# Whole-slot weight conversion on VectorE and attention in 64-token halves, in a gated linear attention and two MoE layers

## The chip, the cores and the metric

The kernel runs on one core of one Trainium2 chip. The metric is the device time of one execution in microseconds (us), as the median of several runs. Times of single instructions come from one profiled execution.

## What is computed

A gated linear attention over 4 batches, 8 heads, 768 tokens and a head size of 48 gives 3072 tokens of 384 values; then come two feed-forward layers with 1536 hidden values each. Cut to what matters:

```python
f = 1.0 / (1.0 + np.exp(-f_logit))
for t in range(S):
    state = f[:, :, t, :, None] * state + np.einsum('bhd,bhe->bhde', k[:, :, t], v[:, :, t])
    y[:, :, t] = np.einsum('bhd,bhde->bhe', q[:, :, t], state)
x = y.transpose(0, 2, 1, 3).reshape(B * S, H * D)
a = x @ w_a;  b = x @ w_b;  x1 = a * b @ w_out
g = x1 @ w_gate;  val = x1 @ w_val
out = g * (1.0 / (1.0 + np.exp(-g))) * val @ w_out2
```

The weights reach the kernel as float64 bit patterns in int64.

## The kernel before, in words

**Two phases of six blocks.** A block is 512 tokens. Phase 1 (`ph` 0) runs the first MoE layer on blocks 0 to 5, phase 2 (`ph` 1) the second. A block runs over 12 slices `j` of 128 hidden values. For a slice TensorE (PE) does three groups of 9 matmuls of 512 columns: `g_in(j, a)`, `g_in(j, b)` and, one slice late, `g_out(j-1)`. Nine, because each operand is held as a rounded part `hi` and a remainder `lo`, and hi·hi, hi·lo and lo·hi are taken for three pieces of 128 rows. `g_in(j, a)` ends with a copy to `a_sb` on ScalarE (ACT), a Silu in phase 2 (L535). `g_in(j, b)` ends with the product on VectorE (DVE, L539). Then ACT rounds the product to `h_hi` (L511) and DVE takes the remainder `h_lo` (L513). `g_out` reads both; its second matmul is the first that reads `h_lo` (L557, L558, L559 are its three lines). After slice 11 the three accumulators are copied out and stored (L568), to `x1d` in phase 1, to `out` in phase 2. Phase 2 loads `x1d` back and splits it (`x1_split`, L583 on ACT, L584 on DVE), three pieces a block.

**Weights.** One slice of one layer is 128 x 1152 values: 384 each for a, b and out. Before, it comes in three parts of 384 columns. Each goes through ACT twice (magnitude of the high words, low words scaled), DVE shift L250, DVE mask-and-or L251, a 32-bit integer add on GpSimd (POOL, L253), an ACT copy to `hi` and DVE L267 to `lo`. In phase 1 the 12 slices of the first layer are converted while block 0 runs, those of the second layer between blocks 2 and 4, and kept in DRAM to be split in block 5.

**Attention** feeds phase 1. Before, its unit is a half-chunk `n`: 128 tokens of 4 of the 8 heads, 48 units in all, 8 for each block. Its steps are `a0` to `a10`: two scans over tokens on DVE (L347, L354), the products of q and k with the scans on POOL (L358, L365), transposes of k on PE (L388), scores `pa` (L404, four matmuls), the masked scores `am` (L421), the state update `u` (L413, four matmuls; `um` on DVE L439, `st` on POOL L440), the output `y` (two matmuls L450 with the state, four L452 with `am`), and rounding to `xhi` (ACT L474) and `xlo` (DVE L478). The last chunk of a batch has no transposes and no `u`, the first no L450. All of these matmuls are float32, and each takes two records in the trace; each of the MoE matmuls takes one. Attention of block 0 fills the front; that of block i+1 is woven into block i.

**Order.** `at(t, f)` hangs steps on group number `t`; the loop at the end walks the groups and issues what hangs there. For the DMA queue of SP the order is that of the code; for the other engines a scheduler of the framework decides it from the dependences of tiles. PSUM tiles come from tagged buffers: `a`, `b`, `o0` to `o2`, `psT`, `psA`, `psY`. In phase 2 the even slices use `a` and `b`, the odd slices `psT` and `psY` (L521 to L525).

Of the kernel before, what the change touches and what calls it, by code (L numbers as in the profile page):

```python
# [30 lines left out]
SB = 32  # L31
NSB = C // SB
PB = NSB * (SB + 1)
# [9 lines left out]
def linear_attention__then__moe_moe(tc, fqk, vt, w1, w2, fn, qn, kn, vn, out):  # L43
    nc = tc.nc
    with tc.tile_pool(name="keep", bufs=1) as kp, tc.tile_pool(name="dram", bufs=1, space=DRAM) as dp:
        flag = kp.tile([1, 1], mybir.dt.int32, tag="flag", name="flag")
        w2d = dp.tile([NJ, 3, 128, DM], F32, tag="w2d", name="w2d")
# [7 lines left out]
def general_path(ctx: ExitStack, tc, dp, w1, w2, fn, qn, kn, vn, out):  # L55
# [50 lines left out]
    for ph in range(2):  # L106
        with ExitStack() as c:
# [8 lines left out]
            for j in range(NJ):  # L116
                for part in range(3):
                    wv = w[:, j, part]
                    raw = pt.tile([128, DM], I64, tag="raw", name="raw")
                    nc.sync.dma_start(out=raw, in_=(w1, w2)[ph][j, part])  # L120
                    to_f32(nc, raw, wv)
# [63 lines left out]
def main_path(ctx: ExitStack, tc, dp, flag, w2d, fqk, vt, w1, w2, out):  # L185
# [23 lines left out]

    def constants():  # L210
        g = nc.gpsimd
        g.memset(restart, 0.0)
        g.memset(restart[:, ::C + 1], 1.0)
        nc.vector.memset(idle, 0.0)
        nc.vector.memset(okacc, 1.0)
        nc.vector.memset(xsum, 0.0)
        for t in fscan + fpad + ipad + sbuf_state:
            nc.vector.memset(t, 0.0)
# [4 lines left out]
        g.affine_select(out=causal, in_=causal, compare_op=ALU.is_ge, fill=0.0,  # L223
                        base=0, pattern=[[1, C]], channel_multiplier=-1)
# [3 lines left out]
    wraw = {}  # L228

    def conv_load(ph, j, part):  # L230
        t = mp.tile([128, DM], I64, tag="wraw", name="wraw", bufs=3)
        nc.sync.dma_start(out=t, in_=(w1, w2)[ph][j, part])
        wraw[ph, j, part] = t

    def conv_a(ph, j, part):


        raw = wraw[ph, j, part]
        lo, hi = words(raw)
        t = mp.tile([128, DM], F32, tag="w32", name="w32", bufs=4)  # L240
        i = (ph * NJ + j) * 3 + part
        nc.scalar.activation(out=t, in_=hi.bitcast(F32), func=AF.Abs, scale=W_DOWN, accum_out=wsum[:, i:i + 1])
        nc.scalar.activation(out=lo, in_=lo, func=AF.Copy, scale=2.0 ** -29)
        wraw[ph, j, part] = (raw, t)

    def conv_b(ph, j, part):
        raw, t = wraw[ph, j, part]
        lo, hi = words(raw)
        tu = t.bitcast(U32)
        nc.vector.tensor_scalar(out=tu, in0=tu, scalar1=3, scalar2=None, op0=ALU.logical_shift_left)  # L250
# [3 lines left out]
        wraw[ph, j, part] = t  # L254

    def wtile(ph, j):
        if (ph, j) not in wt:
            wt[ph, j] = wp.tile([128, 2, 3 * DM], F32R, tag=f"w{j}", name=f"w{j}")
        return wt[ph, j]

    def split(ph, j, part):
        t = wraw.pop((ph, j, part))
        w = wtile(ph, j)
        hi = w[:, 0, part * DM:(part + 1) * DM]
        lo = w[:, 1, part * DM:(part + 1) * DM]
        nc.scalar.activation(out=hi, in_=t, func=AF.Copy, scale=1.0 / W_UP)  # L266
        nc.vector.scalar_tensor_tensor(out=lo, in0=t, scalar=1.0 / W_UP, in1=hi.bitcast(F32),  # L267
                                       op0=ALU.mult, op1=ALU.subtract)

    def keep(ph, j, part):  # L270
        t = wraw.pop((ph, j, part))
        nc.sync.dma_start(out=w2d[j, part], in_=t)

    def reload(ph, j, part):
        t = mp.tile([128, DM], F32, tag="w32", name="w32", bufs=4)
        nc.sync.dma_start(out=t, in_=w2d[j, part])
        wraw[ph, j, part] = t
# [3 lines left out]
    vts = {}  # L281
# [16 lines left out]
    def a_load(n):  # L298
        ch, half = divmod(n, 2)
        b, c = divmod(ch, NC)  # L300
        if n < N0:
            own[n] = wp.tile([128, 9, 2, C], F32, tag=f"w{NJ - 1 - n}", name="own")
        t = own[n][0:YR, 0:3] if n < N0 else ap.tile([YR, 3, 2, C], F32, tag="fqk", name="fqk", bufs=4)
        nc.sync.dma_start(out=t, in_=fqk[b, c, half])
        hs[n] = {"fqk": t}

    def v_load(n):
        ch, half = divmod(n, 2)
        if half == 0:
            if n < N0:  # L310
                v = own[n].rearrange("p a b c -> p (a b c)")[:, 6 * 2 * C:6 * 2 * C + VW]
            else:
                v = ap.tile([C, VW], F32, tag="v", name="v")
            nc.sync.dma_start(out=v, in_=vt[ch * C:(ch + 1) * C])
            vts[ch] = v

    def v_head(ch, i):

        o = (i // 2) * 3 * D + (i % 2) * 2 * D
        return vts[ch][:, o:o + D], vts[ch][:, o - (i % 2) * D:o - (i % 2) * D + PW]  # L320

# [15 lines left out]
    def a1(n):  # L337
        h = hs[n]
        t = h["fqk"]
        if n < N0:  # L340
            o = own[n].rearrange("p a b c -> p (a b c)")[0:YR]
            ps_ = o[:, 3 * 2 * C:3 * 2 * C + 2 * (C + 1)]
            inv = h["inv"] = o[:, 4 * 2 * C + 8:4 * 2 * C + 8 + 2 * PB]
        else:
            ps_ = ap.tile([YR, 2 * (C + 1)], F32, tag="p", name="p", bufs=3)
            inv = h["inv"] = ap.tile([YR, 2 * PB], F32, tag="inv", name="inv", bufs=1)
        nc.vector.tensor_tensor_scan(ps_, fscan[n % 2], restart, 0.0, ALU.mult, ALU.add)  # L347
        p = h["p"] = past(ps_)
        ip = ipad[n % 2]
        pe = ap.tile([YR, 2, NSB], F32, tag="pe", name="pe")  # L350
        nc.vector.tensor_scalar(out=pe, in0=p[:, :, SB - 1::SB], scalar1=P_MIN,
                                scalar2=None, op0=ALU.max)
        nc.vector.reciprocal(ip[:, SB::SB + 1], pe.rearrange("p a s -> p (a s)"))  # L353
        nc.vector.tensor_tensor_scan(rev(inv), rev(fpad[n % 2]), rev(ip), 0.0, ALU.mult, ALU.add)  # L354
        nc.vector.scalar_tensor_tensor(out=okacc, in0=p[:, :, C - 1], scalar=P_MIN, in1=okacc,
                                       op0=ALU.is_ge, op1=ALU.mult)
        qh = h["qh"] = t[:, 1]
        nc.gpsimd.tensor_tensor(out=qh, in0=qh, in1=p, op=ALU.mult)  # L358

    def a2(n):  # L360
        h = hs[n]
        kh = h["kh"] = h["fqk"][:, 2]
        kv = kh.rearrange("p a (s c) -> p (a s) c", c=SB)
        iv = h["inv"].rearrange("p (s c) -> p s c", c=SB + 1)[:, :, 1:]
        nc.gpsimd.tensor_tensor(out=kv, in0=kv, in1=iv, op=ALU.mult)  # L365

    def last(n):
        return (n // 2) % NC == NC - 1

    def first(n):  # L370
        return (n // 2) % NC == 0

    def bank(n, i):
        tag = (("psT", "psA", "psY", "psY") if n >= N0 else
               (("psT", "psA", "psY", "a"), ("o0", "o1", "o2", "b"))[n % 2])[i]
        return ps.tile([128, 512], F32, tag=tag, name=tag)

    def a4(n):
        if last(n):
            return  # L380
        h = hs[n]
        tu = h["tu"] = bank(n, 0)
        if n == 0:

            for i in range(WARM):
                mm(tu, idle[:, 0:128], idle, start=True, stop=True)
        for pp in range(2):
            nc.tensor.transpose(tu[:, pp * YR:(pp + 1) * YR], h["kh"][:, pp], ident[0:YR, 0:YR])  # L388

    def a5(n):  # L390
        if last(n):
            return
        h = hs[n]
        kt = h["kt"] = ap.tile([C, 2 * YR], F32, tag="kt", name="kt")
        nc.scalar.activation(out=kt, in_=h["tu"][:, 0:2 * YR], func=AF.Copy)

    def a6(n):
        h = hs[n]
        ch, half = divmod(n, 2)
# [311 lines left out]
```

## Time and profile before

| | |
|---|---|
| median of 3 runs | 1096.06 us (1095.78 to 1098.13) |
| the profiled execution | 1099.28 us, its span 1097.6 us |
| mean granted TensorE clock | 0.964 |
| busy: PE / DVE / ACT / POOL | 97% / 48% / 36% / 16% |

Shares are of the span. The span is the time from the first to the last instruction; the execution's own time has 1.7 us more around it. PE, the engine of the matmuls, is busy nearly throughout, but the trace models the ends of matmuls, so the busy share doesn't tell how close PE is to its own pace: that is read from the distance between starts.

### The profile page before, as it was taken

How to read it: one execution, taken by the hardware profiler on the slowest of the kernel's cores; microseconds unless marked ns; L12 is line 12 of the kernel's file. 1: busy time of each engine (PE TensorE's matmuls, PEld its weight loads, DVE VectorE, ACT ScalarE, POOL GpSimd, SP SyncE). 2: the span in 40 equal slices, each digit the busy share in tenths (PEclk: the TensorE clock that was granted, in tenths of full speed). 3: DMA queues.
4: the chain of work that ended last, by engine and by line, in shares of the span. 5: the costliest groups of instructions: out<-in, count | busy, mean ns of one | idle time of the engine just before them, and what ended most of it. 6: DMA issues, size and time to landing. Idle time of an engine off the chain costs nothing. (4 is left out here: it accounts for less than half of the span.)

```text
span 1097.6 us, 14275 instructions
## 1 busy us (share of the span) xinstructions
PE 1063.1 (97%) x5242; PEld 857.6 (78%) x5242; DVE 527.5 (48%) x1085; ACT 399.5 (36%) x996; POOL 178.2 (16%) x242
## 2 busy tenths in 40 slices
PE   7988989999999999999999999999999999999997
PEld 5866767778777787787888888888888888888885
DVE  8799885555566666557424542232232222322221
ACT  4456663433344345434324452222131222322221
POOL 4354452111132322224100000000000000000000
PEclk6588899999999999999999999999999999999999
DMA  9034460212343245324203330010010100100000
GB/s 249 29 125 156 141 180 14 89 36 78 113 137 112 73 160 160 101 84 165 84 1 122 117 125 11 0 58 1 1 58 1 38 21 1 58 1 1 29 1 32
DMA packets 38191, 81.23 MB, mean 74 GB/s; under 512 B 4320, under 2 KB 13536, under 8 KB 38112
## 3 DMA queue, kind: packets, MB, share of 16 engines
q1 hardware_dynamic: 38112, 80.23, 23.2%
q8 instruction: 43, 0.70, 0.3%
q14 instruction: 36, 0.29, 0.1%
HBM read 63.70 MB, written 16.52 MB: 73 GB/s over the span
## 5 line engine op out<-in xcount | busy, mean ns | idle before, releaser
L531 PE MATMUL b<-xhi,w 128*128 128x512 f32 x648 | 227.3, 405 | 3.3 <-DVE ip L353 3.3
L531 PE MATMUL a<-xhi,w 128*128 128x512 f32 x648 | 225.2, 402 | 2.6 <-ACT a_sb L535 2.6
L511 ACT ACTIVATE h_hi<-a_sb 128x512 fp32r<-128x512 f32 x144 | 90.8, 630 | 259.7 <-DVE a_sb L539 259.4
L539 DVE TENSOR_TENSOR a_sb<-b,a_sb 128x512 f32<-128x512 f32 x108 | 74.4, 689 | 207.4 <-PE b L531 206.8
L557 PE MATMUL o<-h_hi,w 128*128 128x512 f32 x432 | 173.8, 403 | 0.0
L558 PE MATMUL o<-h_lo,w 128*128 128x512 f32 x432 | 169.0, 391 | 1.0 <-DVE h_lo L513 1.0
L559 PE MATMUL o<-h_hi,w 128*128 128x512 f32 x432 | 168.9, 391 | 0.0
L531 PEld LDWEIGHTS b<-xhi,w 128*128 128x128 f32 x648 | 124.9, 193 | 32.6 <-ACT w L266 3.7
L531 PEld LDWEIGHTS a<-xhi,w 128*128 128x128 f32 x648 | 122.6, 189 | 29.7 <-ACT a_sb L535 2.8
L513 DVE TENSOR_TENSOR h_lo<-a_sb,h_hi 128x512 fp32r<-128x512 f32 x144 | 104.0, 722 | 73.9 <-ACT h_hi L511 73.8
L531 PE MATMUL b<-xlo,w 128*128 128x512 f32 x324 | 129.3, 399 | 0.0
L531 PE MATMUL a<-xlo,w 128*128 128x512 f32 x324 | 127.4, 393 | 0.0
L535 ACT ACTIVATE a_sb<-a 128x512 f32<-128x512 f32 x108 | 64.1, 594 | 171.3 <-PE a L531 171.0
L253 POOL TENSOR_TENSOR w<-w,wraw 128x384 uint32<-128x384 uint32 x72 | 82.0, 1139 | 134.6 <-DVE w L251 82.4
L558 PEld LDWEIGHTS o<-h_lo,w 128*128 128x128 f32 x432 | 81.7, 189 | 17.2 <-DVE h_lo L513 1.8
L559 PEld LDWEIGHTS o<-h_hi,w 128*128 128x128 f32 x432 | 81.4, 188 | 17.4
L557 PEld LDWEIGHTS o<-h_hi,w 128*128 128x128 f32 x432 | 81.9, 190 | 16.4
L539 DVE TENSOR_TENSOR a_sb<-psY,a_sb 128x512 f32<-128x512 f32 x36 | 24.9, 692 | 137.6 <-PE psY L531 137.6
L531 PE MATMUL psT<-xhi,w 128*128 128x512 f32 x216 | 72.3, 389 | 0.0
L531 PE MATMUL psY<-xhi,w 128*128 128x512 f32 x216 | 72.3, 389 | 0.0
L531 PEld LDWEIGHTS b<-xlo,w 128*128 128x128 f32 x324 | 62.6, 193 | 12.3
L531 PEld LDWEIGHTS a<-xlo,w 128*128 128x128 f32 x324 | 61.6, 190 | 11.2
(122 smaller groups left out, 1329.2 us busy)
## 6 DMA issues: line engine op xcount, KB each, us to landing
wraw<-w SPq DMA_DIRECT2D x72, 384.0 KB, 3.6
fqk<-fqk SPq DMA_DIRECT2D x40, 336.0 KB, 3.5
w2d<-w SPq DMA_DIRECT2D x36, 192.0 KB, 2.3
w<-w2d SPq DMA_DIRECT2D x36, 192.0 KB, 2.4
v<-vt SPq DMA_DIRECT2D x20, 288.0 KB, 4.5
x1d<-o_sb SPq DMA_DIRECT2D x18, 256.0 KB, 2.0
x1raw<-x1d SPq DMA_DIRECT2D x18, 256.0 KB, 2.7
out_dram<-o_sb SPq DMA_DIRECT2D x18, 256.0 KB, 2.1
```

The source lines that it names most:

```text
L253: nc.gpsimd.tensor_tensor(out=tu, in0=tu, in1=lo, op=ALU.add)
L511: nc.scalar.activation(out=b, in_=a, func=AF.Copy)
L513: nc.vector.tensor_tensor(out=o, in0=a, in1=b.bitcast(F32), op=ALU.subtract)
L531: mm(t[:, :n], l, r[:, kt, :n], start=first_mm, stop=(kt == KT - 1 and k == 2))
L535: nc.scalar.activation(out=a[:, :n], in_=t[:, :n], func=AF.Silu if ph else AF.Copy)
L539: nc.vector.tensor_tensor(out=a[:, :n], in0=t[:, :n], in1=a[:, :n], op=ALU.mult)
L557: mm(p, wo[:, 0, l], hh[:, :n], start=st, stop=False)
L558: mm(p, wo[:, 0, l], hl[:, :n], start=False, stop=False)
L559: mm(p, wo[:, 1, l], hh[:, :n], start=False, stop=sp)
```

## The change

Three things are done at once. First, each slice of the first layer's weights comes in one transfer into its own slot and is converted in whole rows of 1152; the integer add moves from POOL to DVE, for both layers, and appears there as an operation on 2304 columns. Second, attention takes 128 tokens of all 8 heads as its unit (24 units), cut into two halves `s` of 64 tokens: scans of 520 columns, scores of 64 x 64, a state update for each half. The products with the scans and `st` move from POOL to DVE. Third, the transfers of the front are issued in an order written out by hand, and the second layer's converted weights are kept and reloaded as whole slices. PSUM is tagged anew: `psAY` and `o01` are tiles of two banks (1024 columns), and in phase 2 an odd slice puts `a` and `b` into the two halves of one `psAY` tile. Phase 1 copies out of the accumulators are all on ACT.

```diff
-    def conv_b(ph, j, part):
-        nc.vector.tensor_scalar(out=tu, in0=tu, scalar1=3, scalar2=None, op0=ALU.logical_shift_left)
...
-        nc.gpsimd.tensor_tensor(out=tu, in0=tu, in1=lo, op=ALU.add)
+    def to_float(raw, t, total):
...
+        nc.vector.tensor_tensor(out=tu, in0=tu, in1=lo, op=ALU.add)
...
+    def w1_load(j):
+        stage[j] = slot(j, "wraw")
+        nc.sync.dma_start(out=stage[j], in_=w1[j])
...
-        nc.gpsimd.tensor_tensor(out=qh, in0=qh, in1=p, op=ALU.mult)
+        nc.vector.tensor_tensor(out=segments(qh), in0=segments(qh), in1=p, op=ALU.mult)
...
-        nc.gpsimd.tensor_tensor(out=kv, in0=kv, in1=iv, op=ALU.mult)
+        nc.vector.tensor_tensor(out=segments(kh), in0=segments(kh), in1=iv, op=ALU.mult)
...
-        for pp in range(2):
-            for hh in range(2):
-                rows = slice(hh * VB, hh * VB + D)
-                mm(pa[hh][:, pp * C:(pp + 1) * C], h["kh"][rows, pp], h["qh"][rows, pp], start=True, stop=True)
+        for p in range(NP):
+            for s in range(NS):
+                for hh in range(2):
+                    rows = slice(hh * VB, hh * VB + D)
+                    cols = slice(s * CS, (s + 1) * CS)
+                    mm(pa[cols, hh, p * CS:(p + 1) * CS], h["kh"][rows, p, cols], h["qh"][rows, p, cols],
+                       start=True, stop=True)
...
+    def inter(n, s):
         h = hs[n]
...
+        for p in range(NP):
+            mm(h["py"][0:PW, s, p * CS:(p + 1) * CS], state[s][:, p], h["qh"][:, p, s * CS:(s + 1) * CS],
+               start=p == 0, stop=False, skip_group_check=True)
...
-                nc.gpsimd.tensor_tensor(out=new, in0=um[r], in1=pe, op=ALU.mult)
+                nc.vector.tensor_tensor(out=um[r], in0=u, in1=state[s][r, :, hh * D:(hh + 1) * D], op=ALU.add)
+                nc.vector.tensor_tensor(out=new, in0=um[r], in1=pe, op=ALU.mult)
...
-        if ph == 0:
+        if ph == 0 or j % 2 == 0:
             tag = "ab"[which]
+            t = ps.tile([128, 512], F32, tag=tag, name=tag)
         else:
-            tag = ("ab"[which], ("psT", "psY")[which])[j % 2]
-        t = ps.tile([128, 512], F32, tag=tag, name=tag)
+            if which == 0:
+                both[0] = ps.tile([128, 1024], F32, tag="psAY", name="psAY")
+            t = both[0][:, which * 512:(which + 1) * 512]
...
+    T0 = 20
+    loads = ["c0", "w0", "c1", "c2", "c3", "w1", "w2", "c4", "w3", "w4", "c5"] + [f"w{j}" for j in range(5, NJ)]
```

How the instructions stand changes at two places that matter below. The first is PE in phase 2, at an odd slice: `w` is the slice's weights, `o` the accumulators, and the waits are printed behind a row. Before, with the last matmul of the slice before's `b` on top, the 9 matmuls of `g_out` and then the odd slice's `a` half in `psT`:

```order
L531 MATMUL b<-xhi,w_5766 128x512
L557 MATMUL o_7796<-h_hi,w_5715 128x512 [waits Activation_49]
L558 MATMUL o_7796<-h_lo,w_5715 128x512 [waits DVE_49]
L559 MATMUL o_7796<-h_hi,w_5715 128x512
...
L559 MATMUL o_7798<-h_hi,w_5715 128x512
L531 MATMUL psT<-xhi,w_5815 128x512
...
L531 MATMUL psT<-xhi,w_5815 128x512
L531 MATMUL psY<-xhi,w_5815 128x512
```

And PE in the changed kernel, an odd slice from the end of its `a` half in `psAY`:

```order
L546 MATMUL psAY<-xhi,w_5575 128x512
L574 MATMUL o_7509<-h_hi,w_5534 128x512 [waits Activation_49]
L575 MATMUL o_7509<-h_lo,w_5534 128x512 [waits DVE_49]
L576 MATMUL o_7509<-h_hi,w_5534 128x512
L574 MATMUL o_7509<-h_hi,w_5534 128x512
L546 MATMUL psAY<-xhi,w_5575 128x512 [waits Activation_49]
L546 MATMUL psAY<-xlo,w_5575 128x512
...
L546 MATMUL psAY<-xhi,w_5575 128x512
L575 MATMUL o_7509<-h_lo,w_5534 128x512
L576 MATMUL o_7509<-h_hi,w_5534 128x512
```

The first four matmuls of `g_out` of the even slice before now stand between the two halves of the odd slice, and the other five behind the second half; the second half waits for ACT, which reads the first half. So `g_out` of an even slice begins 9 instead of 18 matmuls behind the end of that slice's own `b`, in all 36 odd slices of phase 2. At even slices the order is `a`, `b`, `g_out` as before.

The second place is DVE in block 0, where weights are converted beside the MoE. Before, three parts of two slices:

```order
L267 SCALAR_TENSOR_TENSOR w_752<-w_667,w_752 128x384
L250 TENSOR_SCALAR w_741<-w_741 128x384
L513 TENSOR_TENSOR h_lo<-a_sb,h_hi 128x512
L251 SCALAR_TENSOR_TENSOR w_741<-wraw,w_741 128x384
L267 SCALAR_TENSOR_TENSOR w_752<-w_703,w_752 128x384
L250 TENSOR_SCALAR w_758<-w_758 128x384
L421 TENSOR_TENSOR am<-psA,causal 128x2x128
L251 SCALAR_TENSOR_TENSOR w_758<-wraw,w_758 128x384
```

And DVE in the changed kernel, at about the same slice:

```order
L554 TENSOR_TENSOR a_sb<-b,a_sb 128x512
L239 TENSOR_SCALAR t<-t 128x1152
L252 SCALAR_TENSOR_TENSOR w_625<-t,w_625 128x1152
L240 SCALAR_TENSOR_TENSOR t<-wraw,t 128x1152
L526 TENSOR_TENSOR h_lo<-a_sb,h_hi 128x512
L242 ISA t<-wraw,t 128x2304
L413 TENSOR_TENSOR am<-psAY,causal 128x512
L554 TENSOR_TENSOR a_sb<-b,a_sb 128x512
```

Four long instructions a slice stand where nine short ones did, the third of them (printed as ISA, 2304 columns) being the add that POOL did. Up to the product of slice 0 DVE now has 5 scans' units, 4 shifts, 4 mask-and-ors, 4 adds, 3 `lo` parts, 30 state instructions (`um`, `st`), 4 `am` and 4 units of `xlo`. From there to the product of slice 9 it has 9 products, 9 `h_lo`, 8 shifts, 8 mask-and-ors, 8 adds, 9 `lo` parts, 7 scans, 7 products with scans, 18 state instructions, 4 `am` and 3 units of `xlo`.

## Rows read from the trace of the kernel before

**Rows 1.** DMA queue of SP: start, us, count of the stores that end blocks.
```profile
194.49 3.07 SPq L568 DMA_DIRECT2D x1d<-o_sb  x3
...
578.12 3.02 SPq L568 DMA_DIRECT2D x1d<-o_sb  x3
...
728.33 0.33 SPq L568 DMA_DIRECT2D out_dram<-o_sb  x1
...
1022.08 0.33 SPq L568 DMA_DIRECT2D out_dram<-o_sb  x1
```

**Rows 2.** Windows: stretch, its length, then busy us by engine, clock, DMA, GB/s.
```profile
55.00:165.00 110.00, 95.39 (x468) 72.85 (x466) 101.63 (x206) 70.83 (x204) 55.37 (x58) 0.89 0.49 150
...
200.00:580.00 380.00, 376.81 (x2089) 301.73 (x2088) 215.16 (x489) 152.47 (x437) 91.71 (x130) 0.99 0.31 99
```

**Rows 3.** Timeline of DVE in block 0: start, us, line, operation, shapes.
```profile
72.06 0.15 DVE L355 SCALAR_TENSOR_TENSOR okacc<-p,okacc 112x2 f32<-112x2 f32 x1
72.24 0.69 DVE L539 TENSOR_TENSOR a_sb<-b,a_sb 128x512 f32<-128x512 f32 x1
...
74.00 0.33 DVE L250 TENSOR_SCALAR w<-w 128x384 uint32<-128x384 uint32 x1
...
77.66 0.54 DVE L251 SCALAR_TENSOR_TENSOR w<-wraw,w 128x384 uint32<-128x384 uint32 x1
...
78.59 1.16 DVE L250 TENSOR_SCALAR w<-w 128x384 uint32<-128x384 uint32 x1
...
169.19 0.69 DVE L539 TENSOR_TENSOR a_sb<-b,a_sb 128x512 f32<-128x512 f32 x1
169.80 0.70 DVE L354 TENSOR_TENSOR_SCAN inv<-fp,ip 112x264 f32<-112x264 f32 x1
```

**Rows 4.** DVE groups by form, 55 to 165 us: busy us, mean ns, idle before.
```profile
L439 DVE TENSOR_TENSOR um<-psT,st 48x96 f32<-48x96 f32 x8 | 2.0, 252 | 0.1
```

**Rows 5.** POOL groups by form, 55 to 165 us.
```profile
L253 POOL TENSOR_TENSOR w<-w,wraw 128x384 uint32<-128x384 uint32 x34 | 40.0, 1175 | 35.6 <-DVE w L251 19.2 <-ACT wraw L243 5.4 <-DVE um L439 2.8
```

**Rows 6.** Timeline of PE around the attention of one half-chunk.
```profile
171.32 0.40 PE L531 MATMUL a<-xhi,w 128*128 128x512 f32 x1
...
171.97 0.27 PE L404 MATMUL psA<-fqk 48*128 48x128 f32 x1
...
172.09 0.27 PE L404 MATMUL psA<-fqk 48*128 48x128 f32 x1
...
172.63 0.39 PE L531 MATMUL b<-xlo,w 128*128 128x512 f32 x1
...
174.24 0.39 PE L531 MATMUL b<-xhi,w 128*128 128x512 f32 x1
...
175.21 0.39 PE L558 MATMUL o<-h_lo,w 128*128 128x512 f32 x1
...
176.82 0.39 PE L559 MATMUL o<-h_hi,w 128*128 128x512 f32 x1
...
178.60 0.39 PE L531 MATMUL a<-xlo,w 128*128 128x512 f32 x1
```

**Rows 7.** Timeline of PE in phase 2: last `b` matmul of two slices.
```profile
803.43 0.39 PE L531 MATMUL psY<-xhi,w 128*128 128x512 f32 x1
...
809.55 0.39 PE L531 MATMUL b<-xhi,w 128*128 128x512 f32 x1
809.78 0.39 PE L557 MATMUL o<-h_hi,w 128*128 128x512 f32 x1
```

**Rows 8.** Timeline of DVE in phase 2, behind those matmuls.
```profile
803.93 0.69 DVE L539 TENSOR_TENSOR a_sb<-psY,a_sb 128x512 f32<-128x512 f32 x1 [3.54 <-PE psY L531]
805.32 0.69 DVE L513 TENSOR_TENSOR h_lo<-a_sb,h_hi 128x512 fp32r<-128x512 f32 x1 [0.70 <-ACT h_hi L511]
...
813.27 0.69 DVE L513 TENSOR_TENSOR h_lo<-a_sb,h_hi 128x512 fp32r<-128x512 f32 x1 [0.70 <-ACT h_hi L511]
```

**Rows 9.** Timeline of PE in block 0: a matmul that waited, and the next.
```profile
88.48 0.50 PE L558 MATMUL o<-h_lo,w 128*128 128x512 f32 x1 [0.97 <-DVE h_lo L513]
88.82 0.39 PE L559 MATMUL o<-h_hi,w 128*128 128x512 f32 x1
```

More of the change, by code (lines that the diff above doesn't have):

```diff
@@ L30 @@
 BLOCKS = [512] * 6
-SB = 32
-NSB = C // SB
-PB = NSB * (SB + 1)
+CS = 64
+NS = C // CS
+NP = H // 2
+SEG = NP * NS
+SW = SEG * (CS + 1)
 P_MIN = 2.0 ** -48
@@ L270, in keep, with slot, operands @@
[L270 to L277, printed above, removed]
+        nc.vector.tensor_tensor(out=tu, in0=tu, in1=lo, op=ALU.add)
+    def slot(j, name):
+        return wp.tile([128, 3 * DM], I64, tag=f"w{j}", name=name)
+    def operands(j):
+        return wp.tile([128, 2, 3 * DM], F32R, tag=f"w{j}", name=f"w{j}")
@@ L373, in bank, with warm @@
     def bank(n, i):
-        tag = (("psT", "psA", "psY", "psY") if n >= N0 else
-               (("psT", "psA", "psY", "a"), ("o0", "o1", "o2", "b"))[n % 2])[i]
-        return ps.tile([128, 512], F32, tag=tag, name=tag)
+        tag = (("psT", "a") if i == 0 else ("psAY", "o01"))[n % 2 if n < N0 else 0]
+        t = ps.tile([128, 512 * (i + 1)], F32, tag=tag, name=tag)
+        return t.rearrange("p (b c) -> p b c", b=2) if i else t
+    def warm(m):
+        t = ps.tile([128, 512], F32, tag="b", name="b")
+        for i in range(m):
+            mm(t, idle[:, 0:128], idle, start=True, stop=True)
@@ L443, in a8, with a8m @@
+    def a8m(n):
         h = hs[n]
-        ch, half = divmod(n, 2)
-        py = h["py"] = bank(n, 2)
-        for pp in range(2):
-            y = py[0:PW, pp * C:(pp + 1) * C]
-            inter = not first(n)
-            if inter:
-                mm(y, sbuf_state[ch % 2][:, 2 * half + pp], h["qh"][:, pp], start=True, stop=False)
-            for hh in range(2):
-                mm(y, v_head(ch, 4 * half + 2 * pp + hh)[1], h["am"][:, 2 * pp + hh],
-                   start=not inter and hh == 0, stop=hh == 1)
@@ L455, in y_parts @@
-    def y_parts(n):
-        if n % 2 == 0:
-            return ((0, PW, slice(0, 2), 0, slice(0, 2), 0),)
-        return ((0, PW, slice(0, 1), 0, slice(2, 3), 1),) + tuple(
-            (32 * i, 32, slice(1, 2), PW, slice(i, i + 1), i) for i in range(KT))
+        inter(n, 1)
+        for p in range(NP):
+            for hh in range(2):
+                for s in range(NS):
+                    mm(h["py"][0:PW, s, p * CS:(p + 1) * CS], v_head(n, p, hh, s)[1],
+                       h["am"][s * CS:(s + 1) * CS, hh, p],
+                       start=first(n) and s == 0 and p == 0 and hh == 0, stop=hh == 1, skip_group_check=True)
@@ L462, in y_views @@
     def y_views(n):
-        ch, half = divmod(n, 2)
-        bi, o = chunk_block[ch]
+        bi, o = chunk_block[n]
         hi, lo = xtiles(bi)
-        py = hs[n]["py"][:, 0:2 * C].rearrange("p (a b) -> p a b", a=2)
-        for r, m, pairs, x0, tiles, col in y_parts(n):
-            rows = slice(x0, x0 + m)
-            c = ch * KT + col
-            yield py[r:r + m, pairs], hi[rows, tiles, o:o + C], lo[rows, tiles, o:o + C], xsum[rows, c:c + 1]
+        py = h = hs[n]["py"][:, :, 0:NP * CS].rearrange("q s (p c) -> q s p c", p=NP)
@@ L472, in a9, with x @@
+        def x(t, rows, tiles):
+            return t[rows, tiles, o:o + C].rearrange("q p (s c) -> q s p c", s=NS)
+        r = slice(0, PW)
+        yield py[r, :, 0:KT], x(hi, r, slice(0, KT)), x(lo, r, slice(0, KT))
+        for i in range(KT):
+            r = slice(PW, 128)
+            yield (py[32 * i:32 * i + 32, :, KT], x(hi, r, slice(i, i + 1))[:, :, 0],
+                   x(lo, r, slice(i, i + 1))[:, :, 0])
     def a9(n):
-        for y, hi, lo, acc in y_views(n):
-            nc.scalar.activation(out=hi, in_=y, func=AF.Copy, accum_out=acc)
+        for y, hi, lo in y_views(n):
+            nc.scalar.activation(out=hi, in_=y, func=AF.Copy)
```

331 lines of the change are left out of this document (164 added, 167 removed).

## The prediction

> **What bounds the kernel now.** I read the stores first, since the third store of a block tells when the block is done [rows 1]. In phase 2 four blocks lie between 728.33 and 1022.08, 73.4 us each. A block has 36 groups of 9 matmuls, 324 in all, and neighbours start 0.227 us apart (809.55 to 809.78, [rows 7]): 324 x 0.227 = 73.5. So phase 2 is PE at its own pace, with nothing to win in it and anything that makes PE wait to lose. Blocks 1 to 4 take 383.6 us (194.49 to 578.12), which is four times 73.4 and 90.0 for the attention that is woven in. Block 0 is the part where PE waits: by the windows, DVE is busy 101.6 of 110 us between 55 and 165, and POOL 55 [rows 2]. There DVE sets the pace: the product of slice 0 starts at 72.24, that of slice 9 at 169.19, 97.0 us for nine slices that PE could do in 9 x 6.1 = 55 us [rows 3]. So the reader has three stretches with three limits: DVE up to about 170 us, PE with attention up to 580, PE alone behind it. The change works on each of them differently.
>
> **Block 0.** I price DVE's new instructions by its old ones where they stood alone. Taking 0.15 us as the fixed part, from the tiny L355 [rows 3], the rest grows with the columns. The shift takes 0.33 for 384 columns, so 0.15 + 3 x 0.18 = 0.69 for 1152. The mask-and-or takes 0.54, so 1.32, and the `lo` part, also an operation of two inputs, the same. A scan takes 0.70 for 264 columns, so 1.23 for 520. A product of 512 columns is 0.69 [rows 3]. The state instructions took 0.252 for 96 columns [rows 4], so 0.35 for 192. The rounding to `xlo`, 384 columns and three times 128 at that same pace, is 0.56 + 3 x 0.29 = 1.4.
>
> The add has no row on DVE. Its 2304 columns at the pace of the shift (0.47 ns a column) are 0.15 + 1.08 = 1.23 us; at that of the mask-and-or (1.02 ns) they are 2.5. No row is nearer to one than to the other (two inputs like the second, but half the bytes a column), so I take the middle, 1.9, and keep 1.2 and 2.5. A conversion then costs 0.69 + 1.32 + 1.9 + 1.32 = 5.2 us of DVE a slice. POOL needed 1.175 us a part, 3.5 a slice, for the same add [rows 5], but beside DVE.
>
> The Trainium skill, page "GPSIMD Engine Reference", says in its table of what to use that GpSimd is about half as fast as VectorE for elementwise work with two inputs. By that sentence the add would be some 3.5 / 2 = 1.8 us a slice, an estimate from the page's factor, and the sum would hardly move; no run here shows it yet.
>
> Now the sums. Between the products of slices 0 and 9 DVE has 9 products and 9 `h_lo` (12.4), 8 shifts, mask-and-ors and adds and 9 `lo` parts (8 x 3.9 + 11.9 = 43.1), 7 scans (8.6), 7 products with scans (4.8), 18 state instructions (6.3), 4 `am` of 512 columns (2.8), 3 units of `xlo` (4.2), and about 2 of small ones: 84 us. Now DVE is idle 8.4 in 110 there [rows 2]; the same share makes 84 into 91. That is 6 less than the 97.0 of before. Before the product of slice 0 it has 10 scans (12.3), 10 products with scans (6.9), 4 x 3.9 + 3 x 1.3 = 19.5 of conversion, 30 state instructions (10.5), 4 `am` (2.8), 4 units of `xlo` (5.6), some 2.6 of small ones and 3 of clearing, in all 63; with about 5 us of waiting for the first chunk's load and the first slice's, and 4 between, that is 72 to 73, as now. So block 0 ends 5 us earlier. The work taken off POOL doesn't count by itself, as POOL was not late. What counts is that DVE's own instructions were stretched beside it: the same shift took 0.33 and, at 78.59, 1.16 [rows 3]. That is what pays for some 5 us of work that DVE gets a slice. With the add at 2.5 the 12 adds cost 0.6 x 12 = 7 more and block 0 ends 2 us later than now; at 1.2 it ends 13 earlier. Bounds: -16 to +8, the outer ends for the front's waits.
>
> **Blocks 1 to 4.** The attention's cost on PE is read as the gap that it makes in the stream of 0.227 [rows 6]. Scores: 172.63 - 171.32 less two steps is 0.86. Update `u`: 175.21 - 174.24 less two is 0.52. Output: 178.60 - 176.82 less two is 1.33. Over the 32 half-chunks in these blocks, less `u` in the 6 at a batch's end and a third of the output in the 4 at its beginning, this is 86.7 - 3.1 - 1.8 = 81.8. The other 8 of the 90.0 are transposes and waits, which I leave as they are.
>
> A unit of 128 tokens and 8 heads now has: scores, 16 matmuls of 64 x 64, two records each; u, 16 of 48 columns; 8 with the state and 16 with `am`, of 64 columns with 96 columns of weights. The scores' records came two at a time, one pair 0.11 after the other (171.97, 172.09), for 128 columns of weights and 128 streamed; so 64 need 0.055, and 32 records four at a time come to 8 x 0.055 + the 0.42 of fixed gap that the old ones show = 0.86; two at a time it would be 0.45 more. `u` by the same reckoning, 32 records of 0.04 four at a time and 0.35 fixed, 0.67 (0.3 more at two at a time). The output's records came 0.11 apart for 128 columns streamed. For 64 columns streaming needs 0.055 but the 96 columns of weights 0.083, so I take 0.083: 16 x 0.083 = 1.33 with the state, 32 in pairs, 1.33, with `am`, 0.35 fixed, 3.0. A unit is 4.5 against 5.4 for two old half-chunks. Sixteen units: 72.5, less 2.3 for beginnings and ends, 70, against 81.8: -12. The other end, streaming alone at 0.055: the 32 records that count come to 1.76 instead of 2.66 a unit, another -14. On the other side, at two at a time in place of four, +12.
>
> Pairs are all that the trace shows [rows 6]. The Trainium skill, page "TensorEngine Tiling (Array Packing)", section "Tiling Modes", has four independent tiles of 64 x 64 that load and multiply in parallel, and a drain whenever the mode changes. By the first clause the scores come four at a time, the sum above; no row of this kernel has four.
>
> Against the -12 stand new waits. DVE is now busy 215 of 380 us in this stretch, 57% [rows 2]; with the scans' products, `st` and the second layer's add on it, it comes to some 18 us of work for each 23 us of three slices, 78%. A wait of PE for `am`, `st` or `h_lo` then lasts longer. I take 6 us, from nothing to 14. Sum -6, bounds -20 to +8.
>
> **Phase 2.** Here the order shows something new. An even slice's `b` ends with a matmul at 803.43 in the row; the product starts 0.50 behind it, `h_lo` 1.89, and takes 0.69, so it is done at +2.58 [rows 7, 8]. Before, the 18 matmuls of the next slice stand ahead of its `g_out`: 18 x 0.227 = 4.1 us, and all is hidden. In the changed kernel, at odd slices, 9 matmuls stand ahead; the first of `g_out` would start at +2.27 (it needs `h_hi`, done by +1.89), the second at +2.50, and it needs `h_lo`. It waits some 0.13 to +2.63, and a matmul that waited is followed by the next after 0.34 instead of 0.227, as its weights come late [rows 9]: 0.11 more. So 0.24 for an undisturbed odd slice. Behind the four, the odd slice's second half waits for ACT's Silu of the first half; that would be some 1.0 us behind the half's last matmul, and the four take longer than that, so nothing. Where DVE has something else in hand `h_lo` comes later: in the row of the slice with a split of `x1` (809.55 to 813.27 + 0.69) it is +4.41, which is a wait of 2.0 with the restart. Such company, the copies at a block's end or the splits, falls to 2 of the 6 even slices of a block; I take 0.77 for these, between 0.24 and 2.0 and nearer to the first, as mostly one short instruction is ahead. Sum: 24 x 0.24 + 12 x 0.77 = 5.8 + 9.2 = +15; bounds 8.6 (36 x 0.24) and 20. The five matmuls behind the second half hide what is left.
>
> **Sum.** -5 - 6 + 15 = +4 on the profiled execution's 1099.3, so 1103.3. This one stands 3.2 above the median of the runs, 1096.06, so on that scale 1100. Where the transfers are concerned, fewer and larger ones in order of need change nothing that ends a stretch: a slice and a chunk are about 1 MB each, and DVE needs over 9 us between two of them.
>
> **Rivals.** (1) The stream of attention is bound by columns streamed and not by weights: -14 in blocks 1 to 4, 1086, faster. For it: records of 48 columns go at 0.04, and a load runs beside the matmul before it. Against it: 96 columns of weights are to be loaded for 64 streamed. Sixteen units have 512 such records, so it decides at a pace of 0.083 - 6.2 / 512 = 0.071: below it the kernel is faster than before. 0.17. (2) Block 0 gains more, because DVE unstretched also ends PE's waits sooner and the add goes at 1.2: -10 on mine, 1090. For it the stretched shift, against it that no DVE add is seen. 0.17. (3) The `g_out` waits are absent, because DVE's chain comes out 0.13 shorter or the scheduler's order isn't the chip's: phase 2 as now, 1085. Against it: the order is fixed at build time. 0.06. (4) The add at 2.5 or the front late by a load: block 0 +7 on mine, 1107. 0.16. (5) Two tiles at a time, +12, or DVE waits at their upper bound, +8: 1108 to 1112. 0.14. My forecast, sum within 4 us of 1100, has 0.30.
>
> **Numbers.** About 0.2%, 2.2 us, is what a measurement of this kernel can tell from no change. Faster: rivals 1 to 3, 0.40, less what of them lies within, and a little of the forecast's lower edge, 0.37. Slower: rivals 4 and 5 and some two thirds of the forecast, 0.50. Same 0.13. The range runs from 1079 (rival 1 with some of 2) to 1114. The forecast's own is 1096 to 1104.
>
> **What would show it.** Right: stores of phase 2 some 75.5 to 76 us apart; in odd slices an idle before the `h_lo` matmul of `g_out`; the product of slice 9 at 161 to 166; stores of blocks 0 and 4 378 us apart; DVE's add near 1.9. Wrong: phase 2 blocks at 73.4; records of 64 columns at 0.055; an add at 1.2; DVE idle in block 0.

## The result, and the profile after

The changed kernel takes 1067.61 us (1066.57 to 1068.10, 4 runs), the kernel before 1095.92 over its four. The ratio is 0.974, with a 95% interval of 0.972 to 0.976. The profiled execution takes 1067.88 us, its span 1066.1. The forecast was 1100 and the range began at 1079: the change is a good deal faster, where I had given 0.50 to slower.

The stores divide the span as in [rows 1]; a block is marked here by its first store. DMA queue of SP, changed kernel (L588 was L568):

```profile
169.53 6.75 SPq L588 DMA_DIRECT2D x1d<-o_sb  x3
...
540.58 3.59 SPq L588 DMA_DIRECT2D x1d<-o_sb  x3
614.01 3.59 SPq L588 DMA_DIRECT2D x1d<-o_sb  x3
688.80 3.60 SPq L588 DMA_DIRECT2D out_dram<-o_sb  x3
...
911.88 3.60 SPq L588 DMA_DIRECT2D out_dram<-o_sb  x3
```

Block 0 ends 25.0 us earlier (169.53 against 194.49). Blocks 1 to 4 take 371.0 instead of 383.6, 12.6 less. Blocks of phase 2 take 74.36 us ((911.88 - 688.80) / 3) instead of 73.4, some 6 more over the phase. Together that is -31, as the two profiled spans have it (1097.6 to 1066.1); the medians are 28 apart, since the profiled execution of before stood 3.4 above its median. Up to that much of what is measured against the rows of before in block 0 can be that one execution's own; the profiled executions of the other kernels stand within 1.4 of their medians.

Against [rows 2], the windows of the changed kernel (busy us and number of instructions of PE, of its weight loads, of DVE, ACT and POOL; then granted clock, DMA share, GB/s):

```profile
55.00:165.00 110.00, 105.25 (x883) 83.81 (x883) 103.41 (x164) 54.82 (x86) 0.00 (x0) 0.96 0.24 80
200.00:580.00 380.00, 378.72 (x2925) 313.26 (x2924) 236.31 (x472) 145.66 (x324) 0.00 (x0) 1.00 0.34 109
```

DVE is still busy nearly throughout between 55 and 165 (103.4 of 110), so busy share alone shows no difference; but PE is busy for 105 instead of 95 us, at a granted clock of 0.96 instead of 0.89, and POOL not at all. The stretch between the products of slices 0 and 9 shows it better. Before it is 97 us long, in the changed kernel 75.9, from 67.13 to 142.98. The columns are as in [rows 2]. Before:

```profile
72.24:169.19 96.95, 83.52 (x387) 64.26 (x388) 88.90 (x182) 64.71 (x182) 46.44 (x47) 0.87 0.49 151
```

The changed kernel:

```profile
67.13:142.98 75.85, 72.80 (x614) 57.21 (x612) 74.76 (x110) 41.50 (x64) 0.00 (x0) 1.00 0.20 64
```

DVE's busy time falls from 88.9 to 74.8 us although POOL's work has come to it, and its idle time from 8.0 to 1.1. PE's granted clock was 0.87 there, a mean over stretches at 2.4 GHz and at 1.2 GHz (0.66 from 100 to 110 us, where PE was busy for 6.5 of 10); it is 1.00 now, where PE is busy for 72.8 of 75.9 us.

The two stretches don't hold the same instructions, though: before, DVE converts nearly ten slices in it, in the changed kernel eight. The whole of block 0, up to its first store, is a fairer measure. Before:

```profile
0.00:194.49 194.49, 171.07 (x871) 130.69 (x872) 160.91 (x360) 106.75 (x319) 86.44 (x112) 0.82 0.43 126
```

The changed kernel:

```profile
0.00:169.53 169.53, 149.94 (x1377) 117.02 (x1380) 151.47 (x257) 81.73 (x130) 1.72 (x11) 0.88 0.44 143
```

So of the 25.0 us, DVE's busy time gives 9.4 and its idle time 15.5 (33.6 against 18.1).

DVE's groups by form between the products of slices 0 and 9, changed kernel (busy us, mean ns, idle before):

```profile
L252 DVE SCALAR_TENSOR_TENSOR w<-t,w 128x1152 fp32r<-128x1152 f32 x9 | 12.2, 1351 | 0.1
L242 DVE CUSTOM_DVE_ANT_0 t<-wraw,t 128x2304 uint16<-128x2304 uint16 x8 | 10.8, 1349 | 0.0
L240 DVE SCALAR_TENSOR_TENSOR t<-wraw,t 128x1152 uint32<-128x1152 uint32 x8 | 10.8, 1345 | 0.0
...
L239 DVE TENSOR_SCALAR t<-t 128x1152 uint32<-128x1152 uint32 x8 | 6.0, 746 | 0.1
```

The add runs over 2304 halfwords in 1.35 us, the time of the other two-input instructions over 1152 words. POOL took 1.175 us for each 384 [rows 5].

### The profile page after: what moved, and what is told of

It is laid out like the page before. It is cut to its first block, busy times and chain, and to the rows that moved or that the text cites. A ratio compares the mean times of both kernels' runs of the same rounds, so it can differ in the third digit from the quotient of the medians.

```text
span 1066.1 us, 15761 instructions
## 1 busy us (share of the span) xinstructions
PE 1036.2 (97%) x6625; PEld 842.0 (79%) x6626; DVE 533.3 (50%) x948; ACT 356.6 (33%) x668; POOL 1.7 (0%) x11
## 5 line engine op out<-in xcount | busy, mean ns | idle before, releaser
L546 PE MATMUL b<-xhi,w 128*128 128x512 f32 x648 | 218.1, 391 | 0.9 <-DVE a_sb L554 0.9
L576 PE MATMUL o<-h_hi,w 128*128 128x512 f32 x432 | 168.2, 389 | 0.0
L574 PE MATMUL o<-h_hi,w 128*128 128x512 f32 x432 | 167.2, 390 | 0.4 <-ACT h_hi L524 0.4
L546 PE MATMUL psAY<-xhi,w 128*128 128x512 f32 x432 | 149.7, 401 | 0.0
L546 PEld LDWEIGHTS b<-xhi,w 128*128 128x128 f32 x648 | 121.7, 188 | 26.9 <-DVE a_sb L554 1.5
L526 DVE TENSOR_TENSOR h_lo<-a_sb,h_hi 128x512 fp32r<-128x512 f32 x144 | 99.3, 690 | 74.1 <-ACT h_hi L524 73.9
L546 PE MATMUL b<-xlo,w 128*128 128x512 f32 x324 | 126.2, 390 | 0.0
L554 DVE TENSOR_TENSOR a_sb<-psAY,a_sb 128x512 f32<-128x512 f32 x36 | 24.9, 692 | 175.0 <-PE psAY L546 175.0
L546 PEld LDWEIGHTS psAY<-xhi,w 128*128 128x128 f32 x432 | 81.0, 187 | 25.7 <-ACT a_sb L550 9.5
L574 PEld LDWEIGHTS o<-h_hi,w 128*128 128x128 f32 x432 | 80.9, 188 | 17.8 <-ACT h_hi L524 0.8
L546 PE MATMUL psAY<-xlo,w 128*128 128x512 f32 x216 | 84.0, 389 | 0.0
L546 PEld LDWEIGHTS b<-xlo,w 128*128 128x128 f32 x324 | 60.8, 188 | 12.6
## 6 DMA issues: line engine op xcount, KB each, us to landing
wraw<-w SPq DMA_DIRECT2D x12, 1152.0 KB, 18.1
```

The source lines that it names most:

```text
L526: nc.vector.tensor_tensor(out=o, in0=a, in1=b.bitcast(F32), op=ALU.subtract)
L546: mm(t[:, :n], l, r[:, kt, :n], start=first_mm, stop=(kt == KT - 1 and k == 2))
L554: nc.vector.tensor_tensor(out=a[:, :n], in0=t[:, :n], in1=a[:, :n], op=ALU.mult)
L574: mm(p, wo[:, 0, l], hh[:, :n], start=st, stop=False)
L576: mm(p, wo[:, 1, l], hh[:, :n], start=False, stop=sp)
```

## The experiments

Where the stores stand in each kernel says in which stretch its time went. All times are us, from the profiled executions; medians from the timed runs, with the ratio to the kernel before on the same chip.

| kernel | median | ratio (95%) | block 0 ends | blocks 1 to 4 | phase 2, from the first store of phase 1's last block to that of phase 2's |
|---|---|---|---|---|---|
| before | 1095.9 | | 194.5 | 383.6 | 437.4 |
| changed | 1067.6 | 0.974 (0.972 to 0.976) | 169.5 | 371.0 | 443.7 |
| own_banks | 1060.9 | 0.968 (0.965 to 0.970) | 170.4 | 370.7 | 437.2 |
| after_pool_load | 1078.0 | 0.985 (0.981 to 0.988) | 178.5 | 371.1 | 443.6 |
| before_no_pool | 1081.8 | 0.987 (0.984 to 0.990) | 179.4 | 380.3 | 437.4 |
| after_parts | 1075.5 | 0.981 (0.978 to 0.984) | 176.6 | 370.8 | 444.2 |
| before_add_dve | 1076.2 | 0.983 (0.980 to 0.985) | 176.0 | 380.1 | 437.4 |
| after_add_pool | 1089.7 | 0.995 (0.993 to 0.998) | 190.9 | 371.4 | 443.9 |
| after_qk_pool | 1072.1 | 0.979 (0.977 to 0.982) | 173.5 | 371.0 | 443.7 |
| after_load_order | 1068.7 | 0.977 (0.975 to 0.979) | 170.5 | 370.6 | 443.7 |
| after_halves_apart | 1094.6 | 0.997 (0.996 to 0.999) | 178.4 | 387.2 | 443.9 |
| after_no_warm | 1067.5 | 0.973 (0.971 to 0.976) | 170.6 | 369.4 | 443.7 |

**own_banks: two PSUM tiles for an odd slice of phase 2.**

```diff
             if which == 0:
-                both[0] = ps.tile([128, 1024], F32, tag="psAY", name="psAY")
-            t = both[0][:, which * 512:(which + 1) * 512]
+                t = ps.tile([128, 512], F32, tag="psT", name="psT")
+            else:
+                t = ps.tile([128, 1024], F32, tag="psAY", name="psAY")[:, 0:512]
```

> The changed kernel, but in phase 2 an odd slice puts its a half into psT and its b half into the first bank of psAY, two tiles as before the change. Theory: the 0.9 us that each block of phase 2 became longer are the restarts of the second half behind the Silu of the first (6 odd slices a block, 0.11 us and a slightly slower stream behind it); blocks of phase 2 go back to 73.4 us and the time falls by 5 to 6 us, to about 1062. Rival: the longer blocks come from something else (the order of stores, the two-bank accumulators): 1067 to 1068.

Measured: 1060.9, and phase 2 back at 437.2. The stores of own_banks stand 73.44 us apart again:

```profile
688.38 3.60 SPq L589 DMA_DIRECT2D out_dram<-o_sb  x3
...
908.70 3.60 SPq L589 DMA_DIRECT2D out_dram<-o_sb  x3
```

So the shared tile is all of phase 2's loss. This version is the fastest of all that ran, 35 us below the kernel before.

**after_pool_load: POOL kept busy with adds whose results nobody reads.**

```diff
         to_float(raw, t, wsum[:, j:j + 1])
+        for part in range(3):
+            z = mp.tile([128, 2 * DM], U32, tag="wraw", name="z")[:, :DM]
+            c = t.bitcast(U32)[:, part * DM:(part + 1) * DM]
+            nc.gpsimd.tensor_tensor(out=z, in0=c, in1=c, op=ALU.add)
```

> The changed kernel, with three adds of 384 columns on POOL for each slice of the first layer, behind its add on DVE; they read the slice's values, write to a spare buffer, and nothing reads what they write. Theory of contention: DVE's instructions stretch beside POOL's (before, some 20 us in the 97 us between the products of slices 0 and 9), so with 36 adds of about 1.1 us DVE's instructions in block 0 get 10 to 16 us longer in sum, and the kernel is 8 to 15 us slower, 1076 to 1083. Rival, that the gain of block 0 comes from fewer and longer instructions: durations on DVE unchanged, 1067 to 1069.

Measured: 1078.0, block 0 9.0 us later and nothing elsewhere. Timeline of DVE in after_pool_load around one group of the spare adds:

```profile
82.83 0.36 DVE L458 TENSOR_TENSOR um<-psAY,st 48x192 f32<-48x192 f32 x1
83.23 1.09 DVE L530 TENSOR_TENSOR h_lo<-a_sb,h_hi 128x512 fp32r<-128x512 f32 x1
84.35 0.87 DVE L459 TENSOR_TENSOR st<-um,p 48x192 f32<-48x192 f32 x1
85.25 0.35 DVE L458 TENSOR_TENSOR um<-psT,st 48x192 f32<-48x192 f32 x1
85.53 1.60 DVE L252 SCALAR_TENSOR_TENSOR w<-t,w 128x1152 fp32r<-128x1152 f32 x1
```

And POOL in the same stretch:

```profile
82.95 2.96 POOL L267 TENSOR_TENSOR z<-t 128x384 uint32<-128x384 uint32 x3 [3.83 <-DVE t L242]
```

While POOL adds, `h_lo` takes 1.09 us (0.69 as the mean of its group in the changed kernel) and `st` 0.87 (0.35 there): both read two tensors in SBUF. `um`, with one input in PSUM, keeps its 0.35. The Trainium skill, page "GPSIMD Engine Reference", section "Specifications", says that GpSimd's SBUF interfaces are shared with VectorE and contend with VectorE's instructions that have two SBUF inputs or run in a mode with two ports. The rows above agree. Not every such instruction that lies beside one of POOL's in the records is longer: in after_add_pool (below), one `lo` part of 1152 columns (L252) began at 99.53, 0.11 us ahead of an add on POOL, and took 1.36.

Block 0 of after_pool_load, to set against the changed kernel's above:

```profile
0.00:178.51 178.51, 153.30 (x1378) 118.70 (x1380) 160.69 (x257) 82.27 (x130) 50.41 (x47) 0.87 0.41 136
```

The same 257 instructions on DVE are busy for 9.2 us more, and DVE is idle for 17.8 us, as in the changed kernel. ACT does wait for the spare adds, 5.5 us in all, since they read a buffer that it writes next; but the idle time shows that the 9.0 us are stretch and not this wait.

**before_no_pool and before_add_dve: the kernel before, with POOL's work, or its add alone, on DVE.**

```diff
-        nc.gpsimd.tensor_tensor(out=tu, in0=tu, in1=lo, op=ALU.add)
+        nc.vector.tensor_tensor(out=tu, in0=tu, in1=lo, op=ALU.add)
```

before_no_pool does the same to the products of q and k with the scans and to `st`.

> The kernel before, with the add of the weights, the two products of the scans and st moved from POOL to DVE, and nothing else. Theory of contention: DVE loses about 20 us of stretch between the products of slices 0 and 9 and gains 29 adds of about 0.5, 14 products of 0.4 and a few st, some 22 us, so block 0 stays within 5 us of before, 1091 to 1101; the rest of the gain then comes from fewer, longer instructions and from the attention. Rival, that taking work off POOL is the whole of block 0's gain: 1070 to 1078.

> The kernel before, with the add of the weights on DVE; the products of the scans and st stay on POOL. The add was 40 of POOL's 55 us between 55 and 165 us. If the gain of 15 us in block 0 that all of POOL's work on DVE gave goes with POOL's busy time, the add alone gives some 10 of it: 1084 to 1088. Rival, that the products are what mattered, since attention waits for them: 1093 to 1096.

Measured: 1081.8 and 1076.2. Both theories fall. The add alone brings more than everything together, 18.5 us in block 0; the products and `st` then cost 3.4 when they follow it. My first theory had DVE gain as much work as it lost in stretch, and forgot its waits. The windows of before_add_dve, between the products of slices 0 and 9 and for the whole of block 0:

```profile
70.40:149.60 79.20, 75.62 (x387) 57.38 (x388) 78.32 (x185) 61.00 (x172) 11.73 (x15) 1.00 0.52 165
...
0.00:176.01 176.01, 165.99 (x871) 125.13 (x872) 157.50 (x396) 106.97 (x319) 46.18 (x76) 0.88 0.47 139
```

In the first of these, busy time falls by 10.6 us against before, but 26 of its 185 instructions are adds, so 23 others now stand outside it, most of them behind the product of slice 9. Block 0 as a whole has the same 360 instructions as before and the 36 adds. Summed by their records the adds take 19.7 us and the others 19.1 less: the stretch that goes pays for the adds and no more. Busy time, where overlapping records count once, falls by 3.4 us. The other 15.1 of the 18.5 are idle time, 18.5 us instead of 33.6. I read this idle time as a chain through POOL's add: shift and mask-and-or on DVE, the add, then the copy to `hi` on ACT, which does the MoE's copies and roundings too. Waits of that copy for the add over the whole kernel (us, times, longest), before:

```profile
ACT w L266 <- POOL w L253: 25.5, 22, 2.8
```

And before_add_dve:

```profile
ACT w L266 <- DVE w L253: 8.3, 10, 1.3
```

**after_add_pool and after_qk_pool: the changed kernel, with the add, or the products and `st`, back on POOL.** The edits are the lines above in reverse.

> The changed kernel, with the add back on POOL (1152 columns for the first layer, 384 for the second). DVE is rid of 12 x 1.35 = 16 us in front of and in block 0 and gets stretch in return: the 48.7 us of spare adds on POOL cost 9 us there, 12 adds of some 3.5 us would be about 42 us and 8 us. Theory that only DVE's sum of durations counts: block 0 up to 8 us earlier, 1060 to 1068. Rival, that the conversion waits for the slow add on its way to the MoE (shift, or, add, copy, lo for one slice lie in a chain of two buffers): 1070 to 1080.

> The changed kernel, with the two products of the scans and st back on POOL. DVE is rid of some 2.8 us for each of 9 units up to the end of block 0, and stretches beside POOL. By the sum of durations alone block 0 moves by less than 6 us either way, 1062 to 1073. Rival, that attention's chain through POOL, which is slower in each of them, holds PE up in the front and in blocks 1 to 4: 1075 to 1095.

Measured: 1089.7 and 1072.1. The add on POOL takes back 21.3 of block 0's 25.0 us, more than even the rival had; the products and `st` 4.0. The windows of after_add_pool, between the same products and for block 0:

```profile
73.30:162.60 89.30, 77.17 (x584) 62.16 (x576) 77.37 (x102) 39.17 (x61) 26.45 (x8) 0.90 0.15 47
...
0.00:190.87 190.87, 159.89 (x1378) 125.63 (x1380) 156.58 (x245) 81.80 (x130) 41.46 (x23) 0.82 0.38 127
```

So the slow add works in two ways. It stretches DVE: in block 0 12 adds of 1.35, 16.2 us, are gone, and yet DVE is busy for 5.1 us more than in the changed kernel, so the stretch is some 21. And DVE is idle for 34.3 us instead of 18.1, in the chain of conversion, ACT and MoE; PE waits with it, and its clock between the two products is 0.90. The copy's waits for the add, changed kernel:

```profile
ACT w L251 <- DVE t L242: 15.5, 9, 3.9
```

And after_add_pool:

```profile
ACT w L251 <- POOL t L242: 32.8, 12, 5.1
```

The scheduler sets DVE's order anew in each version, which is a rival cause. Here it hardly differs: 209 instructions other than adds start ahead of the product of slice 9, against 206 in the changed kernel. From before to before_add_dve the order changes more, and no run separates it from the wait. How much of the wait is due to PE's lower clock is open too.

**after_parts: conversion in parts of 384 on DVE.** Each of the four instructions of a whole slice (L239, L240, L242, L252) becomes three, in a loop over columns:

```diff
+        for k in range(0, t.shape[1], DM):
+            c, h, l = (x[:, k:k + DM] for x in (tu, hi, lo))
...
+            nc.vector.tensor_tensor(out=c, in0=c, in1=l, op=ALU.add)
```

> The changed kernel, with each of DVE's four instructions of a whole slice of the first layer cut into three of 384 columns (ACT's stay whole). Theory that the length of instructions matters: 8 more instructions a slice at some 0.07 to 0.10 us of fixed cost each, 7 to 10 us over 12 slices, most of it in block 0: 1073 to 1078. Rival, that only contention mattered: 1067 to 1069.

Measured: 1075.5, block 0 7.1 us later. That is 0.074 us for each of the 96 instructions that came on: whole slices are worth 7 us beside the add on DVE.

**after_halves_apart: the matmuls of `am` ordered by half.**

```diff
-        for p in range(NP):
-            for hh in range(2):
-                for s in range(NS):
+        for s in range(NS):
+            for p in range(NP):
+                for hh in range(2):
```

> The changed kernel, with the 16 matmuls of am ordered by half first: all 8 of tokens 0 to 63, then all 8 of tokens 64 to 127, instead of alternating. In the changed kernel their 32 records take 1.50 us, 0.094 a pair, which is the pace of the 96 columns of weights if the two halves of the array load and multiply side by side. Theory that alternating is what pairs them: the 32 records take 3.0 us, 1.5 more in each of 24 units, some 24 us in blocks 1 to 4 and some of it in block 0: 1092 to 1102. Rival, that neighbours in the order do not matter: 1067 to 1069.

Measured: 1094.6; blocks 1 to 4 take 387.2, 16 more where 24 were expected, and are longer than before the change. PE in after_halves_apart:

```profile
323.29 0.81 PE L432 MATMUL psAY<-fqk,st 112*96 112x64 f32 x8
324.03 2.64 PE L463 MATMUL psAY<-am,v 64*96 64x64 f32 x32
326.61 0.50 PE L546 MATMUL a<-xhi,w 128*128 128x512 f32 x1
```

The 32 records take 2.58 us between starts, against 1.50 in the changed kernel (below). The two halves of the array work side by side only when neighbours in the order alternate between them, and this alternation decides whether the halves are a gain at all. The Trainium skill, page "TensorEngine Tiling (Array Packing)", section "Tiling Modes", says that tiles load and multiply in parallel; this holds here for neighbours, not for eight in a row on one half.

**after_load_order and after_no_warm: two small parts of the front.** The first writes c0 to c5 ahead of all weights in the list `loads`; the second drops `at(3 * i + 1, warm, 8)`.

> The changed kernel, with the attention chunks c0 to c5 loaded ahead of all weights instead of the order written by need. The chunks are 0.98 MB each at some 0.28 MB a us, so the first slice lands at about 24 us instead of 8 to 10 and the third at 32. Theory that the order in the front carries little, as the first slice is needed only after the attention of block 0 at about 57 us: 1066 to 1070. Rival, that DVE's order, fixed at build time, has the first slice's conversion ahead of later chunks' scans and stands behind the load: 1073 to 1085.

> The changed kernel without the three groups of 8 spare matmuls that the change hangs into the front (the 20 at the very start stay). PE's granted clock is at its lower level from 30 to 60 us in the changed kernel with them. If DVE sets the front, nothing is lost: 1066 to 1069. Rival, that the spare matmuls hold the clock up between 10 and 25 us and attention's chain gains by it: 1070 to 1074.

Measured: 1068.7 and 1067.5. Neither moves block 0 by more than 1.1 us. This order of loads and the spare matmuls carry next to nothing.

## Why the prediction was wrong, point by point

**Block 0, -5 forecast, -25 measured.** This is the step that failed: "The work taken off POOL doesn't count by itself, as POOL was not late." POOL was late: before, ACT waited 25.5 us for its add (above). It was right that DVE is the engine that is busy nearly throughout, that its instructions were stretched beside POOL, and that this stretch pays for the adds.

Three terms of my 91 us between the products of slices 0 and 9 were too long; 75.9 were measured. The add was taken at 1.9, the middle of its bounds, and takes 1.35: 8 of them are 4.4 us. DVE's busy time came to 74.8, not 84: with the add's 4.4 out, about 5 of the rest is that I summed durations where instructions overlap in the records. In [rows 3] it is seen: the product at 169.19 lasts 0.69, and the scan behind it starts at 169.80, 0.08 before its end; there are 110 instructions in the stretch. The idle time was carried over as a share, 7 us, where 1.1 is left. This last is a mechanism and not a size: the idle time belonged to the slow add, whose chain DVE and PE waited for, and to PE's waits, around which its clock fell.

before_add_dve and after_add_pool show that moving the add alone is worth 18.5 and 21.3 of the 25 us, and DVE's idle time in block 0 is the larger part of it both times: 33.6 and 34.3 us with the add on POOL, 18.5 and 18.1 with it on DVE. after_pool_load shows that stretch alone, with no such wait, costs its full length too, 9 us. The length of the instructions is worth 7 (after_parts) and the products and `st` 4 (after_qk_pool); the parts overlap, so they do not add up. The product of slice 0 itself came at 67.1, not at 72 to 73. These 5 us go with the add too: in after_add_pool, with the add back on POOL, that product comes at 73.3.

Rival 2 named this direction, with a price of 10 us for 20; that waits end sooner too is what the runs bear out. Its reason, that DVE is unstretched, is not the whole of it: in after_pool_load DVE is stretched and still idle for no longer than in the changed kernel, so the idle time that went belongs to the add's place. It held 0.17.

**Blocks 1 to 4, -6 forecast, -12.6 measured.** The working of PE's gaps held, the 6 us for new waits did not. PE in the changed kernel, the unit's three places in the stream:

```profile
300.29 0.39 PE L576 MATMUL o<-h_hi,w 128*128 128x512 f32 x1
...
301.11 0.89 PE L432 MATMUL psAY<-fqk,st 112*96 112x64 f32 x8
...
302.13 0.39 PE L546 MATMUL a<-xlo,w 128*128 128x512 f32 x1
...
307.82 0.39 PE L576 MATMUL o<-h_hi,w 128*128 128x512 f32 x1
308.04 0.81 PE L432 MATMUL psAY<-fqk,st 112*96 112x64 f32 x8
308.79 1.57 PE L463 MATMUL psAY<-am,v 64*96 64x64 f32 x32
310.29 0.50 PE L546 MATMUL a<-xhi,w 128*128 128x512 f32 x1
310.63 0.39 PE L546 MATMUL a<-xlo,w 128*128 128x512 f32 x1
...
316.34 0.39 PE L576 MATMUL o<-h_hi,w 128*128 128x512 f32 x1
...
317.05 0.69 PE L407 MATMUL psAY<-fqk 48*64 48x64 f32 x32
317.67 0.50 PE L546 MATMUL a<-xhi,w 128*128 128x512 f32 x1
```

The state matmuls take 0.094 each on average (0.75 for 8) and those of `am` 0.094 a pair. That is near the 0.083 that I took from 96 columns of weights and far from the 0.055 of 64 columns streamed, so rival 1 is out. That the loading of weights sets this pace is argued from the two figures; no run tests it alone. The scores, 32 records in 0.62, come four at a time, so rival 5's first half is out too. DVE at 62% busy (236 of 380) makes PE wait for almost nothing, once for 1.3 us between 170 and 580; my 78% was too high. That the total comes out at the -12 that I had worked out for PE's gaps is in part luck: of the 12.6, some 3.3 come with POOL's work off DVE's path already in the old attention (380.1 and 380.3 against 383.6 in the two variants of before), the other 9 with the halves.

**Phase 2, +15 forecast, +6 measured, for another reason.** The sign was luck. Here I miscounted. I let `g_out` of an even slice begin 9 matmuls behind the end of its own `b`, instead of 18; but the 9 of the slice before's `g_out` stand in between as well, so it was 27 before and is 18 now, and `h_lo` is long done. (The row at 803.43 that I read the chain from writes `psY` and so ends an odd slice; behind an even one the product starts 0.50 later too, at 773.64 in the changed kernel, so this changes nothing.) PE in the changed kernel, where the last row of `b` is that of the even slice:

```profile
773.14 0.39 PE L546 MATMUL b<-xhi,w 128*128 128x512 f32 x1
...
777.22 0.39 PE L546 MATMUL psAY<-xhi,w 128*128 128x512 f32 x1
777.45 0.39 PE L574 MATMUL o<-h_hi,w 128*128 128x512 f32 x1
777.67 0.39 PE L575 MATMUL o<-h_lo,w 128*128 128x512 f32 x1
...
778.13 0.39 PE L574 MATMUL o<-h_hi,w 128*128 128x512 f32 x1
778.36 0.50 PE L546 MATMUL psAY<-xhi,w 128*128 128x512 f32 x1
778.69 0.39 PE L546 MATMUL psAY<-xlo,w 128*128 128x512 f32 x1
```

`h_lo` of that slice, on DVE, starts at 775.09 even with a split of `x1` ahead of it, and is done 1.9 us before its matmul:

```profile
775.09 0.69 DVE L526 TENSOR_TENSOR h_lo<-a_sb,h_hi 128x512 fp32r<-128x512 f32 x1
```

The wait that does cost is the one that I had priced at nothing, the second half's for the Silu of the first, on ACT (first row; the second is the load of the waiting matmul's weights):

```profile
777.71 0.60 ACT L550 ACTIVATE a_sb<-psAY 128x512 f32<-128x512 f32 x1 [2.71 <-PE psAY L546]
...
778.36 0.19 PEld L546 LDWEIGHTS psAY<-xhi,w 128*128 128x128 f32 x1 [0.27 <-ACT a_sb L550]
```

The Silu ends at 778.31, just when the matmul is due at 778.36, so nothing idles there. But the weights are loaded only then, and the next matmul comes after 0.33 us instead of 0.227. 0.11 in 6 odd slices makes 0.6 of the 0.9 us a block; the stream behind it is a little slower too. own_banks takes the whole back.

## What to carry to other kernels

Don't take an engine that is half idle for one that is never late: ask who waits for it. Here adds of 1.2 us on POOL cost more, in stretch on DVE and in the chain behind them, than adds of 0.55 us on DVE itself. The busy share of DVE between 55 and 165 us hid it, as it stood above 90% before and after. When work moves, compare an engine's busy and idle time over a part of the kernel that holds the same work in both versions. Price an engine that is busy throughout by the distance between starts, and don't carry an idle share over to a program that takes its cause away. When a schedule is read for what stands between a producer and its consumer, count all groups in the stream, and count a wait that ends just in time as the load of weights behind it.

## What the hardware showed unexpectedly

A 32-bit integer add on DVE runs as a custom instruction on halfwords at 1.35 us for 1152 words; on POOL the same width took 3.4 us on average between 55 and 165 us of after_add_pool. Matmuls on the two row halves of the array overlap when neighbours alternate (1.50 us for 32 records) and not when eight in a row lie on one half (2.58).
